# One transformer block in one pass: x^T of four tiles of the second half through VectorE and a DRAM scratch, and a different order on VectorE in the opening

## The chip, the core and the metric

The kernel runs on one core of a Trainium2 chip. A core has TensorE (PE, matmuls and transposes, results in PSUM), VectorE (DVE), ScalarE (ACT), GpSimd (POOL), and SyncE (SP), whose queue issues nearly all DMAs here. Each engine works through its own instructions in program order and waits where an operand is not there yet or a buffer is not free. The metric is the device time of one execution in microseconds (us); the median of three executions before the change is 1181.57 us (1181.06 to 1181.97).

## The reference, cut to what matters

```python
x = A_x                                  # 1 x 2048 x 576, fp32
xn = _layernorm(x)                       # over the 576 columns, eps 1e-5
# A: qkv = xn @ wqkv; 32 heads of 18; row s attends to rows s, s-2, ..., s-14 (8 of them)
# B: relu(xn @ w1) @ w2, 4608 hidden units
return x + softmax_attention(xn) @ wo + relu(xn @ w1) @ w2
```

The products have to hold fp32 accuracy. TensorE is fed in a shorter form (`F32R`), so every operand is split into a high part (the value rounded to F32R) and a low part (the value minus its high part), and a product is the sum high*high + low*high + high*low.

## The kernel before, in words

**Tiling.** Rows of even index are parity 0 and rows of odd index are parity 1 (an offset of 2 stays within a parity). Each parity (`ph`) has 8 tiles `i` of 128 rows; two tiles make a block `tb` of 256 rows. D = 576 columns are 4 pieces of 128 and a rest of 64. `XT[ph, tb]` holds x^T of a block as 9 pieces of 128 partitions: 4 high, 1 mixed (high part of the rest on partitions 0 to 63, its low part on 64 to 127), 4 low. `TERMS` lists the 14 pairs of pieces that a product over D needs.

**Steps.** The MLP is cut into slots: parity, 12 chunks of hidden units, 4 blocks, 3 units of 128 hidden columns, so 144 slots a parity and 288 in all. The main loop has one step per slot `n`. In each, TensorE first does `h_mm(n + 2)` (14 matmuls of 256 columns: hidden units of the slot two ahead), then what the table `todo` has for the step, then `o_mm(n)` (12 matmuls of 288 columns, summed over three slots in the PSUM pair `PO`); then come the entries of `todo_late`. `h_out` makes the relu's high part on ScalarE (`hhi`, L500) and its low part on VectorE (`hlo`, L503). After the third slot of a chunk `o_out` (L544) adds `PO` to the tile of x, which is also the accumulator of the output; after the last chunk the tile is written out (L474). The tables are written by hand, step by step; `run_bg` puts the attention's VectorE work between the steps by a small sum of expected PE and VectorE time.

**x^T by TensorE.** For a tile of x: `load_x` (a DMA), `stats` (bn_stats and two small ones on VectorE, L239 to L243, then `nm` and `rstd` on GpSimd, L244 and L245), `norm` (one VectorE instruction, L260, or two on ScalarE, L257 and L258), `make_xt`: five TensorE transposes of 128x128 or 128x64 into both buffers of the PSUM pool `ps_m` (L274, L275), then high part on ScalarE (L279), low part on VectorE (L282), and the same for the rest (L286, L289). For parity 1 this is spread over steps 129 to 153, with the last chunk of parity 0 starting at slot `e` = 132: tile `i` is loaded at step e - 3 + 2i, its statistics come late in e + 1 + 2i, its norm late in e + 2 + 2i and its transposes in e + 4 + 2i. That is 136, 138, 140 and 142 for tiles 0 to 3. `h_mm` of parity 1 begins in step 142 (slot 144, block 0) and reaches block 1 in step 145.

**The wo path.** The attention's result of a tile is turned without TensorE: `wo_a` transposes 32x32 blocks on VectorE (L430, L431) into `tr` and stores it in four DMAs to the DRAM tile `turned` (L437), so that the order of blocks is put right; `wo_f` fetches it (L444); `wo_s` splits it (L451 to L453); `wo_b` multiplies with wo in `ps_m` and adds to x (L466). For parity 0, tiles 5 to 7 of it are under way in steps 130 to 136; `wo_b` of tile 7 stands in step 136, ahead of the transposes of parity 1's tile 0.

**Weights.** `run_splits(n)` at the start of a step splits what is due (L137 on ScalarE, L139 or L141 on GpSimd or VectorE) and issues the next weight DMA, three ahead, in the same SP queue.

**The opening.** The first slots, and x^T of parity 0's eight tiles, are laid out by hand ahead of the loop, which starts at step 4. Tiles 4 and 5 are transposed around `h_terms(4)` and `h_terms(5)`. The table `HEAD` places tiles 6 and 7: statistics of 6 in step 4, norm of 6 and statistics of 7 late in step 4, norm of 7 in step 5 (both norms on ScalarE), transposes of 6 late in step 5 and of 7 in step 6. Both need both buffers of `ps_m`.

Of the kernel before, what the change touches and what calls it, by code (L numbers as in the profile page):

```python
# [17 lines left out]
P = 128  # L18
# [3 lines left out]
TBN = 256  # L22
# [5 lines left out]
EPS = 1e-5  # L28

UNIT0, UNIT_STEP, WO_AT = 7, 27, 8  # L30
WO_STEPS = (0, 1, 3, 4, 6, 7, 9, 10)
HEADW = (-9, -8, -7, -6, -5, -4)
FIRST = 4
# [2 lines left out]
    (4, 0, 'stats', 6),  # L36
    (4, 1, 'norm', 6, True),
    (4, 1, 'stats', 7),
    (5, 0, 'norm', 7, True),
    (5, 1, 'xt', 6),  # L40
    (6, 0, 'xt', 7),
)
HALO = ((0, 112), (112, 127))
WARM = 24

# [2 lines left out]
def tile_body(ctx: ExitStack, tc: tile.TileContext, x, wqkv, wo, w1, w2, out):  # L48
# [28 lines left out]
    lgp = pool("lgp", 2)  # L77
    smp = pool("smp", 2)
    tmp = pool("tmp", 2)
    turned = pool("turned", 3, space=bass.MemoryType.DRAM)  # L80
    ps_o = pool("ps_o", 2, space=PSUM)
    ps_h = pool("ps_h", 2, space=PSUM)
    ps_m = pool("ps_m", 2, space=PSUM)
# [145 lines left out]
    def stats(ph, i, parts=False):  # L229
        xt = X[ph, i]  # L230
        st = smp.tile([P, 2, 6], F32, name="bst")
        mv = smp.tile([P, 2], F32, name="mv", bufs=4)
        r = smp.tile([P, 1], F32, name="rstd", bufs=4)
        nm = smp.tile([P, 1], F32, name="nm", bufs=4)
        MR[ph, i] = nm, r

        def sums():
            for h in range(2):
                nc.vector.bn_stats(st[:, h, :], xt[:, h * D2 : (h + 1) * D2])  # L239

        def rest():
            nc.vector.bn_aggr(mv, st)
            nc.vector.tensor_scalar(mv[:, 1:2], mv[:, 1:2], EPS, None, op0=ALU.add)  # L243
            nc.gpsimd.tensor_scalar(nm, mv[:, 0:1], -1.0, None, op0=ALU.mult)  # L244
            nc.gpsimd.tensor_tensor(r, mv[:, 1:2], mhalf, op=ALU.pow)  # L245
            dve(700)

        if not parts:
            sums()
            rest()  # L250
        return sums, rest

    def norm(ph, i, act=False):
        nm, r = MR.pop((ph, i))
        xn = tmp.tile([P, 640], F32, name="xn", bufs=3)[:, 0:D]
        if act:
            nc.scalar.activation(xn, X[ph, i], AF.Identity, bias=nm)  # L257
            nc.scalar.activation(xn, xn, AF.Copy, scale=r)  # L258
        else:
            nc.vector.tensor_scalar(xn, X[ph, i], nm, r, op0=ALU.add, op1=ALU.mult)  # L260
            dve(600)
        XN[ph, i] = xn

    def transpose_split(src, hi, mix, lo, bank=None, parts=False):

        if bank is ps_o:
            po = ps_o.tile([P, 2, 512], F32, name="po")
            pa, pb = po[:, 0, :].rearrange("p (k c) -> p k c", k=KT), po[0:DR, 1, 0:P]
        else:
            pa = ps_m.tile([P, KT, P], F32, name="pm")  # L270
            pb = ps_h.tile([P, TBN], F32, name="ph") if bank is ps_h else ps_m.tile([P, P], F32, name="pm")
            pb = pb[0:DR, 0:P]
        for k in range(KT):
            nc.tensor.transpose(pa[:, k, :], src[:, k * P : (k + 1) * P], ident)  # L274
        nc.tensor.transpose(pb, src[:, KT * P : D], ident)  # L275
        t["pe"] += 5 * 0.06

        def high():
            nc.scalar.activation(hi, pa, AF.Copy)  # L279

        def low():
            nc.vector.tensor_tensor(lo, pa, f32(hi), op=ALU.subtract)  # L282
            dve(512)

        def last_high():
            nc.scalar.activation(mix[0:DR], pb, AF.Copy)  # L286

        def last_low():
            nc.vector.tensor_tensor(mix[DR:P], pb, f32(mix[0:DR]), op=ALU.subtract)  # L289
            dve(128)  # L290

        steps = high, low, last_high, last_low
        if not parts:
            for f in steps:
                f()
        return steps

    def make_xt(ph, i, bank=None, parts=False):
        tb, h = divmod(i, 2)
        if h == 0:  # L300
            XT[ph, tb] = xtp.tile([P, 9, TBN], F32R, name="xT")
        d = XT[ph, tb][:, :, h * P : (h + 1) * P]
        xn = XN.pop((ph, i))
        return transpose_split(xn, d[:, 0:4, :], d[:, 4, :], d[:, 5:9, :], bank, parts)


    TERMS = [(k, k) for k in range(KT)] + [(5 + k, k) for k in range(KT)] + [(4, 4)] + [(k, 5 + k) for k in range(5)]


    QO, KK, VV = {}, {}, {}  # L310
# [108 lines left out]

    OT = {}  # L420

    TD = {}

    def wo_a(ph, i):


        assert (ph, i) in ready, (ph, i, len(bg))
        o = QO[ph][:, i, :]
        tr = tmp.tile([P, 640], F32, name="tr", bufs=1)
        nc.vector.transpose(tr[:, 0:D], o)  # L430
        nc.vector.transpose(tr[:, D:640], o[:, KT * P : D])  # L431
        dve(D)
        dve(DR)
        TD[ph, i] = turned.tile([5 * 4, 32, P], F32, name="turned")
        for r in range(4):
            rows = slice(32 * r, 32 * r + 32)
            nc.sync.dma_start(  # L437
                TD[ph, i][:, :, rows].rearrange("g j i -> j g i"),
                tr[rows, :].rearrange("j (g i) -> j g i", i=32),
            )  # L440

    def wo_f(ph, i):
        OT[ph, i] = tmp.tile([P, 5, P], F32R, name="xn", bufs=3)
# [2 lines left out]
    def wo_s(ph, i):  # L446

        r = OT[ph, i]
        z = f32(r)
        d = tmp.tile([P, 5, P], F32R, name="oT", bufs=1)  # L450
        nc.scalar.activation(d, z, AF.Copy)  # L451
        nc.vector.tensor_tensor(r[:, 0:KT], z[:, 0:KT], f32(d[:, 0:KT]), op=ALU.subtract)
        nc.vector.tensor_tensor(d[DR:P, KT], z[DR:P, KT], f32(d[DR:P, KT]), op=ALU.subtract)  # L453
        dve(512)
        dve(128)
        OT[ph, i] = [d[:, k] for k in range(5)] + [r[:, k] for k in range(4)]

    def wo_b(ph, i):
        d, w = OT.pop((ph, i)), WO[ph]
# [56 lines left out]
    def o_mm(n, out=True):  # L516
        ph, c, tb, f = slots[n]
        hi, lo = H.pop(n)
        w = W2[ph, c, f]
        end = n == len(slots) - 1  # L520
        for k in range(2):
            if f == 0:
                PO[k] = ps_o.tile([P, 2, 512], F32, name="po")
            cs = slice(k * P, (k + 1) * P)
            terms = [(j, l, b, h) for j, (l, b) in enumerate(((hi, 0), (hi, 1), (lo, 0))) for h in range(2)]
            if end:
                terms.sort(key=lambda z: z[3])
            for j, l, b, h in terms:
                mm(
                    PO[k][:, h, 0:D2], l[:, cs], w[:, b, h * D2 : (h + 1) * D2],  # L530
                    f == 0 and j == 0, f == C - 1 and j == 2, D2,
                )
        if out:
            o_out(n)
# [23 lines left out]
    def at(n, f, *a):  # L558
        todo.setdefault(n, []).append((f, a))
# [3 lines left out]
    def late(n, f, *a):  # L563
        todo_late.setdefault(n, []).append((f, a))

    plan = []
    for ph in range(NPH):
        b = ph * SPP
        for c in range(NCH):
            for f in range(C):  # L570
                s = b + c * SPC + f
                first = ph == c == 0
                plan.append((HEADW[f] if first else s - 5, w1_task, ((ph, c, f), c * C + f)))
                plan.append((HEADW[3 + f] if first else s - 3, w2_task, ((ph, c, f), c * C + f)))
        for u in range(NU):
            s = b + UNIT0 + u * UNIT_STEP
            plan.append((s - 5, wq_tasks, ((ph, u), u)))
            for i in range(NI):
                at(s + i, qkv_tile, ph, u, i)
            late(s + NI + 1, attention, ph, u)  # L580
        s = b + UNIT0 + NU * UNIT_STEP + WO_AT
        plan.append((s - 8, wo_tasks, (ph,)))
        for i in range(NI):
            z = s + WO_STEPS[i]
            late(z, wo_a, ph, i)
            at(z + 1, wo_f, ph, i)
            late(z + 2, wo_s, ph, i)
            at(z + 3, wo_b, ph, i)
            at(z + 3, done, ph, i)
        if ph + 1 < NPH:  # L590
            e = b + SPP - SPC
            for i in range(NI):
                z = e + 3 + 2 * i
                at(z - 6, load_x, ph + 1, i)
                late(z - 2, stats, ph + 1, i)
                late(z - 1, norm, ph + 1, i)
                at(z + 1, make_xt, ph + 1, i)
    for step, f, a in sorted(plan, key=lambda z: z[0]):
        if f in (wq_tasks, wo_tasks):
            f([step + k for k in range(5)], *a)  # L600
# [56 lines left out]
    make_xt(0, 3, bank=ps_h)  # L657
    o_mm(2, out=False)
    stats(0, 4)
    stats(0, 5)  # L660
    h_mm(3)
    norm(0, 4)
    norm(0, 5)
    h_terms(4, TERMS)
    h4 = h_out(4, parts=True)
# [14 lines left out]
    for n in range(FIRST, len(slots)):  # L680
        run_splits(n)
        m = n + LAG
        if m < len(slots):
            h_mm(m)
        for f, a in todo.pop(n, []):
            f(*a)
        if n >= 0:
            o_mm(n)
        for f, a in todo_late.pop(n, []):
            f(*a)  # L690
        run_bg(M[slots[n][3] if n >= 0 else 0])
    assert not todo and not todo_late and not bg and not tasks and not staged

# [25 lines left out]
```

## Time and profile before

| what | value |
|---|---|
| median of three executions | 1181.57 us |
| profiled execution: time | 1181.42 us |
| profiled execution: span | 1179.7 us |
| TensorE busy | 1171.0 us, 8936 matmuls and transposes |
| VectorE busy | 818.8 us, 1298 instructions |
| ScalarE busy | 301.9 us, 738 instructions |
| GpSimd busy | 47.5 us |
| one TensorE transpose, 128x128 (L274) | 272 ns median |
| block transpose on VectorE, 128x576 (L430) | 778 ns median |
| granted TensorE clock | 1.0 |

A line of the chain of waits has start, length, engine, output tile and line. A line of the timeline has start, length (of the whole group when it ends in x2 and the like), engine, line, operation, output and input, shapes, and in brackets the idle time just before and what ended it. TensorE's matmuls overlap, so the spacing of starts says more of their cost than the length of one.

### The profile page before, as it was taken

How to read it: one execution, taken by the hardware profiler on the slowest of the kernel's cores; microseconds unless marked ns; L12 is line 12 of the kernel's file. 1: busy time of each engine (PE TensorE's matmuls, PEld its weight loads, DVE VectorE, ACT ScalarE, POOL GpSimd, SP SyncE). 2: the span in 40 equal slices, each digit the busy share in tenths (PEclk: the TensorE clock that was granted, in tenths of full speed). 3: DMA queues.
4: the chain of work that ended last, by engine and by line, in shares of the span. 5: the costliest groups of instructions: out<-in, count | busy, mean ns of one | idle time of the engine just before them, and what ended most of it. 6: DMA issues, size and time to landing. Idle time of an engine off the chain costs nothing.

```text
span 1179.7 us, 21695 instructions
## 1 busy us (share of the span) xinstructions
PE 1171.0 (99%) x8936; PEld 1162.3 (99%) x8936; DVE 818.8 (69%) x1298; ACT 301.9 (26%) x738; POOL 47.5 (4%) x70
## 2 busy tenths in 40 slices
PE   8999999999999999999999999999999999999998
PEld 8999999999999999999999999999999999999998
DVE  7427875888687678877673288758777884887752
ACT  5412222131222222321233123121222322222210
POOL 3200000010000000000020000000100000000000
PEclk9999999999999999999999999999999999999999
DMA  5312121130321211355342113030302313113431
GB/s 182 97 34 76 55 61 56 38 108 1 99 58 46 74 48 42 94 129 134 107 148 66 46 53 88 27 83 23 96 22 79 79 34 89 54 30 99 110 99 61
DMA packets 137650, 86.15 MB, mean 73 GB/s; under 512 B 48864, under 2 KB 121312, under 8 KB 137552
## 3 DMA queue, kind: packets, MB, share of 16 engines
q1 hardware_dynamic: 134736, 76.28, 23.7%
q10 hardware_dynamic: 2816, 8.49, 2.5%
q8 instruction: 70, 1.15, 0.4%
q14 instruction: 28, 0.23, 0.1%
HBM read 66.58 MB, written 9.96 MB: 65 GB/s over the span
## 4 chain that ended last, share of the span: by engine, by line
PE 96%; DVE 1%; DMA 1%; ACT 0%; issue 0%; POOL 0%; SPq 0%; DVEq 0%; ACTq 0%; POOLq 0%
PE ph L105 38%; PE po L105 38%; PE pm L105 20%; PE pm L274 0%; DVE bst L239 0%; DMA xn<-turned 0%; DMA x<-in_x 0%; DMA st<-in_wqkv 0%; DMA turned<-tr 0%; DVE pr L395 0%; POOL rstd L245 0%; DVE w2t L141 0%; ACT xn L257 0%; DVE hlo L503 0%; DVE x L550 0%
## 5 line engine op out<-in xcount | busy, mean ns | idle before, releaser
L105 PE MATMUL ph<-xT,w1t 128*128 128x256 f32 x4018 | 509.3, 278 | 0.7 <-ACT xT L279 0.7
L105 PEld LDWEIGHTS ph<-xT,w1t 128*128 128x128 f32 x4018 | 489.1, 188 | 1.1 <-ACT xT L279 1.0
L105 PE MATMUL po<-w2t,hhi 128*128 128x288 f32 x2304 | 400.7, 296 | 0.0
L105 PEld LDWEIGHTS po<-w2t,hhi 128*128 128x128 f32 x2304 | 337.0, 188 | 1.0
L500 ACT ACTIVATE hhi<-ph 128x256 fp32r<-128x256 f32 x287 | 109.9, 383 | 583.4 <-PE ph L105 560.2
L105 PE MATMUL po<-w2t,hlo 128*128 128x288 f32 x1152 | 245.0, 293 | 0.0
L503 DVE SCALAR_TENSOR_TENSOR hlo<-ph,hhi 128x256 fp32r<-128x256 f32 x287 | 120.8, 421 | 169.2 <-ACT hhi L500 168.5
L544 DVE TENSOR_TENSOR x<-po,x 128x576 f32<-128x576 f32 x190 | 142.5, 756 | 67.2 <-PE po L105 64.1
L105 PE MATMUL pm<-wq,xT 128*128 128x432 f32 x896 | 185.5, 358 | 0.0
L105 PEld LDWEIGHTS po<-w2t,hlo 128*128 128x128 f32 x1152 | 183.8, 188 | 0.0
L105 PEld LDWEIGHTS pm<-wq,xT 128*128 128x128 f32 x896 | 163.8, 188 | 5.6
L358 DVE TENSOR_TENSOR pr<-qo,k 128x1152 f32<-128x1152 f32 x64 | 85.8, 1348 | 0.0
L361 DVE TENSOR_REDUCE lg<-pr 128x64 f32<-128x1152 f32 x64 | 84.9, 1342 | 0.0
L388 DVE TENSOR_TENSOR pr<-lg,v 128x1152 f32<-128x1152 f32 x64 | 84.6, 1348 | 0.2
L141 DVE TENSOR_TENSOR w2t<-st,w2t 128x576 fp32r<-128x576 f32 x72 | 54.3, 754 | 40.4 <-ACT w2t L137 40.2
L395 DVE TENSOR_TENSOR pr<-pr 128x288 f32<-128x288 f32 (+1 forms) x128 | 70.4, 598 | 0.1
L141 DVE TENSOR_TENSOR w1t<-st,w1t 128x640 fp32r<-128x640 f32 x70 | 57.3, 818 | 12.1 <-ACT w1t L137 12.0
L137 ACT ACTIVATE w2t<-st 128x576 fp32r<-128x576 f32 x72 | 49.3, 685 | 55.1 <-PE po L105 46.5
L327 ACT ACTIVATE k<-pm 128x144 f32<-128x144 f32 x64 | 18.6, 291 | 146.5 <-PE pm L105 146.5
L137 ACT ACTIVATE w1t<-st 128x640 fp32r<-128x640 f32 x72 | 52.9, 735 | 2.5 <-DMA st<-in_w 2.3
L364 POOL TENSOR_SCALAR_AFFINE_SELECT lg<-lg 1x512 f32<-1x512 f32 x8 | 9.4, 1172 | 836.7 <-DVE lg L361 836.7
L105 PE MATMUL pm<-wq,oT 128*128 128x288 f32 x224 | 35.2, 296 | 0.8 <-ACT oT L451 0.8
(71 smaller groups left out, 444.2 us busy)
## 6 DMA issues: line engine op xcount, KB each, us to landing
st<-in_w SPq DMA_DIRECT2D x72, 288.0 KB, 3.0
st<-in_w SPq DMA_DIRECT2D x72, 256.0 KB, 3.1
st<-in_wqkv SPq DMA_DIRECT2D x32, 216.0 KB, 3.1
turned<-tr SPq DMA_DIRECT2D x64, 80.0 KB, 2.2
xn<-turned SPq DMA_DIRECT2D x16, 320.0 KB, 3.3
st<-in_w SPq DMA_DIRECT2D x144, 32.0 KB, 2.8
x<-in_x SPq DMA_DIRECT2D x15, 288.0 KB, 4.4
out<-x SPq DMA_DIRECT2D x14, 288.0 KB, 2.2
```

The lines of the kernel that those rows point to most:

```text
L105: nc.tensor.matmul(o, l, r, start=start, stop=stop)
L137: nc.scalar.activation(hi, src, AF.Copy)
L141: nc.vector.tensor_tensor(lo, src, f32(hi), op=ALU.subtract)
L327: nc.scalar.activation(k[:, W - 1 + i, :], pq[:, 1, :], AF.Copy)
L358: nc.vector.tensor_tensor(pr[i], q, window(k, i), op=ALU.mult)
L361: nc.vector.tensor_reduce(lg[:, i], pr.pop(i).rearrange(heads, d=Dh), axis=AX.X, op=ALU.add)
L364: nc.gpsimd.affine_select(out=z, in_=z, pattern=[[1, NI], [1, W], [0, HG]], compare_op=ALU.is_ge, fill=-1e9 / scale, base=1 - W, channel_m ...
L388: nc.vector.tensor_tensor(pr[i].rearrange(heads, d=Dh), e, window(v, i).rearrange(heads, d=Dh), op=ALU.mult)
L395: nc.vector.tensor_tensor(o, z[:, 0:n], z[:, n : 2 * n], op=ALU.add)
L500: nc.scalar.activation(hi, pt, AF.Relu)
L503: nc.vector.scalar_tensor_tensor(lo, pt, 0.0, f32(hi), op0=ALU.max, op1=ALU.subtract)
L544: nc.vector.tensor_tensor(acc, PO[k][:, :, 0:D2], acc, op=ALU.add)
```

## The change

Tiles 0 to 3 of parity 1 get their own steps (`XT_STEPS`, relative to e = 132): load, statistics, norm (now two ScalarE instructions, into half of a product buffer `pr`), block transposition on VectorE into the other half with four stores to a DRAM tile, fetch by three DMAs straight into the piece positions of `XT`, and the split in place. The five TensorE transposes of these four tiles go. To let the fetch land in pieces 0 to 3, high and low parts change places in `XT`, and `TERMS` is renumbered; the order of high and low products stays the same. In the opening, `norm(0, 4)` moves ahead of `h_mm(3)`, between the two halves of `stats(0, 5)`; the norm of tile 7 goes from ScalarE in step 5 to VectorE late in step 4; and in step 5 the second of `o_out`'s two additions moves behind the split of tile 6's transposes.

```diff
+XT_STEPS = (
+    (-6, 0, 1, 2, 4, 7),
+    (-5, 1, 2, 3, 5, 8),
+    (-3, 2, 3, 4, 6, 10),
+    (3, 4, 5, 6, 8, 11),
+)
@@
-    (5, 0, 'norm', 7, True),
+    (4, 1, 'norm', 7),
     (5, 1, 'xt', 6),
     (6, 0, 'xt', 7),
 )
+HALVED = 5
@@
-    turned = pool("turned", 3, space=bass.MemoryType.DRAM)
+    turned = pool("turned", 4, space=bass.MemoryType.DRAM)
@@
-        return transpose_split(xn, d[:, 0:4, :], d[:, 4, :], d[:, 5:9, :], bank, parts)
-    TERMS = [(k, k) for k in range(KT)] + [(5 + k, k) for k in range(KT)] + [(4, 4)] + [(k, 5 + k) for k in range(5)]
+        return transpose_split(xn, d[:, 5:9, :], d[:, 4, :], d[:, 0:4, :], bank, parts)
+    TERMS = (
+        [(5 + k, k) for k in range(KT)] + [(k, k) for k in range(KT)] + [(4, 4)]
+        + [(5 + k, 5 + k) for k in range(KT)] + [(4, 9)]
+    )
+
+    def blocks_out(td, tr):
+        for r in range(4):
+            rows = slice(32 * r, 32 * r + 32)
+            nc.sync.dma_start(
+                td[:, :, rows].rearrange("g j i -> j g i"),
+                tr[rows, :].rearrange("j (g i) -> j g i", i=32),
+            )
+
+    def norm_turned(ph, i):
+        nm, r = MR.pop((ph, i))
+        z = prp.tile([P, W, UD], F32, name="pr").rearrange("p w c -> p (w c)")
+        XN[ph, i] = xn, _ = z[:, 0:D], z[:, D : 2 * D]
+        nc.scalar.activation(xn, X[ph, i], AF.Identity, bias=nm)
+        nc.scalar.activation(xn, xn, AF.Copy, scale=r)
+
+    def xt_a(ph, i):
+        xn, tr = XN.pop((ph, i))
+        nc.vector.transpose(tr, xn)
+        dve(D)
+        TD[ph, i] = turned.tile([D // 32, 32, P], F32, name="words")
+        blocks_out(TD[ph, i], tr)
+
+    def xt_f(ph, i):
+        tb, h = divmod(i, 2)
+        if h == 0:
+            XT[ph, tb] = xtp.tile([P, 9, TBN], F32R, name="xT")
+        z, td = f32(XT[ph, tb][:, 0:5, h * P : (h + 1) * P]), TD.pop((ph, i))
+        nc.sync.dma_start(z[:, 0:KT], td[0 : 4 * KT].rearrange("(k c) j i -> (c j) k i", k=KT))
+        for rows in slice(0, DR), slice(DR, P):
+            nc.sync.dma_start(z[rows, KT], td[4 * KT : D // 32].rearrange("c j i -> (c j) i"))
+
+    def xt_s(ph, i):
+        tb, h = divmod(i, 2)
+        d = XT[ph, tb][:, :, h * P : (h + 1) * P]
+        z = tmp.tile([P, 5, P], F32R, name="oT", bufs=1)[:, 0]
+        mix = d[:, 4, :]
+        nc.scalar.activation(d[:, 5:9, :], f32(d[:, 0:4, :]), AF.Copy)
+        nc.vector.tensor_tensor(d[:, 0:4, :], f32(d[:, 0:4, :]), f32(d[:, 5:9, :]), op=ALU.subtract)
+        nc.scalar.activation(z[DR:P], f32(mix[DR:P]), AF.Copy)
+        nc.vector.tensor_tensor(mix[DR:P], f32(mix[DR:P]), f32(z[DR:P]), op=ALU.subtract)
+        nc.scalar.activation(mix[0:DR], f32(mix[0:DR]), AF.Copy)
+        dve(512)
+        dve(128)
@@
             for i in range(NI):
-                z = e + 3 + 2 * i
-                at(z - 6, load_x, ph + 1, i)
...
+                if i >= len(XT_STEPS):
...
+                load, first, second, send, back, parts = (e + k for k in XT_STEPS[i])
+                at(load, load_x, ph + 1, i)
+                late(first, stats, ph + 1, i)
+                late(second, norm_turned, ph + 1, i)
+                late(send, xt_a, ph + 1, i)
+                at(back, xt_f, ph + 1, i)
+                at(parts, xt_s, ph + 1, i)
@@
     stats(0, 4)
-    stats(0, 5)
+    s5 = stats(0, 5, parts=True)
+    s5[0]()
+    norm(0, 4)
     h_mm(3)
-    norm(0, 4)
+    s5[1]()
     norm(0, 5)
     h_terms(4, TERMS)
@@
         if n >= 0:
-            o_mm(n)
+            o_mm(n, n != HALVED)
+        if n == HALVED:
+            o_out(n, (0,))
         for f, a in todo_late.pop(n, []):
             f(*a)
+        if n == HALVED:
+            o_out(n, (1,))
```

`wo_a` now calls `blocks_out` with the same four stores as before, and `wo_s` hands its pieces to `wo_b` in the new numbering.

More of the change, by code (lines that the diff above doesn't have):

```diff
@@ L310, in tile_body @@
+    TD = {}
     QO, KK, VV = {}, {}, {}
@@ L420, in tile_body @@
     OT = {}
-    TD = {}
     def wo_a(ph, i):
@@ L434, in wo_a @@
         TD[ph, i] = turned.tile([5 * 4, 32, P], F32, name="turned")
[L435 to L440, printed above, removed]
+        blocks_out(TD[ph, i], tr)
     def wo_f(ph, i):
@@ L455, in wo_s @@
         dve(128)
-        OT[ph, i] = [d[:, k] for k in range(5)] + [r[:, k] for k in range(4)]
+        OT[ph, i] = [r[:, k] for k in range(KT)] + [d[:, KT]] + [d[:, k] for k in range(KT)]
     def wo_b(ph, i):
@@ L592, in tile_body @@
             for i in range(NI):
-                z = e + 3 + 2 * i
-                at(z - 6, load_x, ph + 1, i)
-                late(z - 2, stats, ph + 1, i)
-                late(z - 1, norm, ph + 1, i)
-                at(z + 1, make_xt, ph + 1, i)
+                if i >= len(XT_STEPS):
+                    z = e + 3 + 2 * i
+                    at(z - 6, load_x, ph + 1, i)
+                    late(z - 2, stats, ph + 1, i)
+                    late(z - 1, norm, ph + 1, i)
+                    at(z + 1, make_xt, ph + 1, i)
+                    continue
+                load, first, second, send, back, parts = (e + k for k in XT_STEPS[i])
[5 more added lines that the diff above has]
+                at(parts, xt_s, ph + 1, i)
     for step, f, a in sorted(plan, key=lambda z: z[0]):
```

## The prediction

> **What bounds the kernel now.** First I read the page: busy shares, chain of waits, DMA issues.
>
> ```profile
> PE 1171.0 (99%) x8936; PEld 1162.3 (99%) x8936; DVE 818.8 (69%) x1298; ACT 301.9 (26%) x738; POOL 47.5 (4%) x70
> ...
> PE 96%; DVE 1%; DMA 1%; ACT 0%; issue 0%; POOL 0%; SPq 0%; DVEq 0%; ACTq 0%; POOLq 0%
> ...
> turned<-tr SPq DMA_DIRECT2D x64, 80.0 KB, 2.2
> xn<-turned SPq DMA_DIRECT2D x16, 320.0 KB, 3.3
> ```
>
> TensorE is busy almost throughout, at a granted clock of 1.0 in every slice, and 96% of the chain is its own. So an instruction less on TensorE is time gained, if nothing that replaces it makes TensorE wait; work on other engines costs nothing until it is late. The last two rows price the detour the four tiles will take: a store of this shape lands 2.2 us after issue, a fetch 3.3 us.
>
> Next, the chain over the end of parity 0 (start, length).
>
> ```profile
> 559.02 1.61 PE ph L105 x14
> ...
> 565.94 1.60 PE ph L105 x14
> ...
> 571.17 0.47 DVE x L466
> ...
> 571.68 0.66 PE pm L274 x4
> 572.33 0.11 PE pm L275
> ...
> 574.03 1.61 PE ph L105 x14
> ...
> 577.23 1.61 PE ph L105 x14
> 578.85 0.44 PE pm L274 x4
> 579.28 0.11 PE pm L275
> ...
> 580.99 1.61 PE ph L105 x14
> ```
>
> Each "ph" line begins a step: 135 at 559.02, 136 at 565.94, 137 at 574.03, 138 at 577.23, 139 at 580.99. Step 137 has no transposes and takes 3.20 us; step 138 has tile 1's and takes 3.76. So five transposes cost 0.56 us on the path, not their listed 5 x 0.27, because they overlap. Steps 135 and 136 hold the same matmuls, but 136 also has tile 0's transposes: 8.09 against 6.92, so these cost 1.17. The extra 0.6 is a wait: the transposes need both `ps_m` buffers, which VectorE's addition of wo's product (L466) still holds.
>
> Last, the opening, VectorE and TensorE by timeline.
>
> ```profile
> 22.46 0.21 DVE L242 BATCH_NORM_AGGREGATE mv<-bst 128x2 f32<-128x12 f32 x1
> ...
> 23.11 1.23 DVE L260 TENSOR_SCALAR xn<-x,nm,rstd 128x576 f32<-128x576 f32 x2
> 24.25 0.75 DVE L544 TENSOR_TENSOR x<-po,x 128x576 f32<-128x576 f32 x1
> 25.12 0.69 DVE L282 TENSOR_TENSOR xT<-pm,xT 128x512 fp32r<-128x512 f32 x1
> ```
>
> ```profile
> 23.83 0.63 PE L274 MATMUL pm<-ident,xn 128*128 128x128 f32 x4 [0.17 <-DVE xn L260]
> ...
> 26.06 0.60 PE L274 MATMUL pm<-ident,xn 128*128 128x128 f32 x4
> ...
> 37.41 0.65 PE L274 MATMUL pm<-ident,xn 128*128 128x128 f32 x4 [0.48 <-DVE xT L282]
> ```
>
> TensorE waits a little for the norm of tile 4 at 23.83, not at tile 5 (26.06), and 0.48 us at tile 7 (37.41), for the low part of tile 6.
>
> **Term 1: the transposes that go.** Tile 0: 1.17. Tiles 1 to 3, by steps 138, 140 and 142 (3.76, 3.75, 3.75 against 3.20): 0.56 + 0.55 + 0.55. Sum -2.83 us, if the new path is hidden. TensorE's next work after `wo_b` of tile 7 is `o_mm(136)`, which uses the other PSUM pool, so tile 0's wait has no successor there.
>
> **What hides the new path.** New work per tile: two ScalarE instructions for the norm (0.78 each, L257 and L258) for one on VectorE (0.58), a block transpose on VectorE (0.78 by L430, the same 576 columns), four stores, three fetches, and one or two short ScalarE copies more. VectorE is 8.5 us busy in the 16 us from 550, ScalarE 2.6. I follow the queues, in the old clock less what is already saved.
>
> - Tile 0: transposed after the split of wo's tile 6, about 560.8 to 561.5. SP issues its stores behind two output DMAs, 562.1 to 564.8 (0.68 each, as the group at 550.17: 2.74 for four); landed at 567. Fetch issued by 571, landed 574.3. Split due in step 139, about 581.
> - Tile 2's norm writes the `pr` buffer that tile 0's stores read, so ScalarE waits until 567, with the `hhi` of slot 138 behind it: ready at 568.9 instead of 567.6. The slot's low part must be done before `h_mm(140)` takes that PSUM buffer at 576.1: some 7 us to spare.
> - Tile 1: stored 567.0 to 569.7, landed 572. Its fetch stands behind tile 2's stores (572.8 to 575.5) in SP's queue, is issued by 576.8 and lands at 580. Split in step 140 (584 to 586); first reader `h_mm(144)` at 588.9 (591.14 less 2.28).
> - Tile 3: its load waits for tile 0's output DMA as before; stores to 582.4, fetch landed 589.7, split at 594, first reader `h_mm(147)` at 599.0.
> - Queued behind these on SP: the weight load of step 139, 578.4 before, about 582.4 to 584.1 now, landed 587. Its split opens step 141 at 585.7, so ScalarE waits some 1.3 us, with `hhi` of slot 143 behind it, which `o_mm(143)` needs near 592. Hidden.
>
> Cost taken: 0. From below nothing is to be gained; from above the bound is the rival of late data.
>
> **Term 2: norm 4 ahead, a loss.** TensorE's wait at 23.83 goes: the transposes of tile 4 follow the matmuls at 23.67 and end at 24.22 in the chain's clock, where they ended at 24.56. But VectorE now does: norm 4 at 22.45 (`rstd` of tile 4 ends at 22.42), `hlo` of slot 3 at 22.95, and only then the aggregate of tile 5 at 23.28 instead of 22.46. GpSimd follows 0.37 later (as 21.30 to 21.67) and takes 0.76 for `nm` and `rstd`: 24.41. Norm 5 starts at 24.44, where it started at 23.75. Behind it stand the first addition of `o_out(2)` (24.94) and the low part of tile 4, 25.62 to 26.31. Tile 5's transposes want `ps_m` at about 25.7 and get it 0.06 later than this: 26.37. Begun after a wait they take 0.65 + 0.11 in the chain (as at 37.41), so `o_mm(3)` starts at 27.13, where it started at 26.77. **+0.36 us.** From below, if norm 5 gates nothing: -0.34.
>
> `rstd` of tile 5 took 0.77 before, beside VectorE's norm 4, against 0.57 for tiles 4, 6 and 7; in the new order VectorE idles while it runs, so I take 0.57. The Trainium skill, "SBUF — State Buffer", section "SBUF: two separate sides", has VectorE and GpSimd share a port pair by an exclusive lock, so that the loser blocks for a whole instruction. That agrees with 0.77 and 1.04 beside VectorE's work; with 0.77 here too the term would be +0.56.
>
> **Term 3: norm 7 to VectorE, additions split around tile 6: a gain.** ScalarE spends 34.51 to 36.1 on norm 7 while tile 6's transposes are finished at 35.2; its high part starts at 36.05, the low part at 36.66, and TensorE gets `ps_m` at 37.41. New: norm 7 on VectorE at 33.93 (`rstd` ends 33.90), in a stretch where VectorE idles 1.48 us. High part of tile 6 at 35.23 to 35.82; on VectorE one addition (34.98 to 35.66), then the low part 35.85 to 36.54. TensorE finishes `h_mm(8)` at 36.68 and goes straight on: 35.15 + 1.61 + 0.55 = 37.31 for the start of `o_mm(6)`, against 38.17. **-0.86 us.** The second addition then ends at 37.6, and `o_mm(6)` needs its buffer at 38.1. If it frees nothing: 0.
>
> **Sum.** -2.83 + 0.36 - 0.86 = -3.33 us. The profiled span 1179.7 would become 1176.4, its time 1181.42 would become 1178.1; that execution lies 0.15 below the median, so for the median **1178.2 us**.
>
> **Rivals.**
>
> - *Norm 5 gates nothing* (tile 4's low part is ready sooner than I place it): -2.83 - 0.34 - 0.86 = -4.03, 1177.5. For it: only 0.6 us decides. Against: VectorE is in order, norm 5 ahead.
> - *Tile 7 still waits*: its slack is 0.1 us, and a stall that moves to the second addition would take the place of the one removed. -2.83 + 0.36 = -2.47, 1179.1.
> - *The new path is a little late*: the tightest reader is `h_mm(144)`, 3 us behind tile 1's split; ScalarE, in order, is stopped by a buffer or a weight load for some us too long. 1 to 4 us of TensorE waiting end between 1179.2 and 1182.2.
> - *Slower: the stores land late.* One mechanism, in step 135: ScalarE stops at tile 2's norm until tile 0's stores have landed, and `hhi` of slot 138 stands behind. With landing time L, ScalarE goes on at 564.8 + L, and needs 1.56 for the norm, 0.38 for `hhi`, VectorE 0.42 for `hlo`, by 576.1: TensorE waits from L = 8.9 us on, and the change is a loss above 8.9 + 3.3 = 12.2. At L = 16 it is 1181.57 - 3.33 + 7.1 = 1185.3. For it: the pieces are short; 48864 packets lie under 512 B already, mostly these stores (2560 a tile by 16 tiles is 40960). Against: 64 such stores landed in 2.2 median, 3.7 at most. The Trainium skill, "VectorE: DVE Perf Modes", section "The three transpose paths", warns that a plain DMA which transposes by strides is 19 times slower than the transposing one, and in "Rules for kernel authors" recommends TensorE for 128x128; by 19 x 2.2, an estimate, L would be 42 and the loss some 30 us. The row speaks against it: the same pattern already lands in 2.2, since the blocks are turned in VectorE.
>
> That the change does not do what it says is hardly open: 20 transposes leave TensorE, 8936 becomes 8916.
>
> **Chances.** Forecast 55%, its own range 1177.8 to 1178.8 (term 2 to 0.56, measurement). Norm 5 gates nothing 13%, tile 7 still waits 12%, path a little late 14%, slower 6%. What this kernel's measurement can tell from no change is about 0.2%, 2.4 us: below 1179.2 is faster, above 1183.9 slower. The first three cases are faster (80%), the fourth nearly all the same (14%), the last slower (6%). For 8 in 10 the range takes the first three and the start of the fourth: 1177.0 to 1180.3.
>
> **What would show it.** Steps 136, 138, 140 and 142 as long as their neighbours (6.92 and 3.20) and no TensorE wait for the split of `xT` from step 142 on: term 1. An idle gap before tile 5's transposes near 26.4, named for tile 4's low part: term 2. Tile 7's transposes directly behind `h_mm(8)`: term 3. I am wrong if TensorE's waits name ScalarE between steps 136 and 147, or if the landing of the new stores is far above 2.2.

## The result, and the profile after

| | before | after |
|---|---|---|
| median of the comparison | 1181.57 us (1180.92 to 1182.19, 22 runs) | 1179.91 us (1179.09 to 1180.99, 22 runs) |
| profiled execution: time, span | 1181.42, 1179.7 us | 1179.64, 1177.8 us |

The kernel is faster by 1.66 us, ratio 0.9986 [0.998, 0.9993]. The forecast was 1178.2, a gain of 3.33: half of it arrived. The time lies inside the forecast's range (1177.0 to 1180.3), outside the likeliest case's own (1177.8 to 1178.8).

The page of the changed kernel, in the lines that answer to those of before:

```profile
PE 1168.6 (99%) x8916; PEld 1159.7 (98%) x8916; DVE 819.5 (70%) x1299; ACT 307.7 (26%) x748; POOL 46.8 (4%) x70
...
PE 93%; DMA 2%; SPq 2%; DVE 2%; issue 0%; ACT 0%; POOL 0%; DVEq 0%; ACTq 0%; POOLq 0%
...
turned<-tr SPq DMA_DIRECT2D x64, 80.0 KB, 2.7
xn<-turned SPq DMA_DIRECT2D x16, 320.0 KB, 3.1
```

The 20 transposes are gone (8916) and TensorE's busy time fell by 2.4 us. But its share of the chain fell from 96% to 93%: transfers and SP's queue now stand in it with 2% each. That is a sign of where to look, not of how much was lost (2% are some 23 us).

The end of parity 0, by TensorE's timeline after the change (the `h_mm` that begins steps 138 to 141, and 144):

```profile
575.63 1.78 PE L113 MATMUL ph<-xT,w1t 128*128 128x256 f32 x14
...
578.83 1.78 PE L113 MATMUL ph<-xT,w1t 128*128 128x256 f32 x14
...
582.03 1.78 PE L113 MATMUL ph<-xT,w1t 128*128 128x256 f32 x14
...
585.23 1.78 PE L113 MATMUL ph<-xT,w1t 128*128 128x256 f32 x14
...
594.83 1.78 PE L113 MATMUL ph<-xT,w1t 128*128 128x256 f32 x14
```

Each step is 3.20 us, the three from 585.23 to 594.83 (9.60) too; steps 138, 140 and 142 took 3.75 before. No wait of TensorE for the split of x^T shows here. What follows step 143, by the chain of waits of the same kernel:

```profile
595.03 0.15 DVE hlo L555
595.18 0.18 issue
595.36 0.68 DVE xT L359
596.08 0.29 DVE xT L361
596.40 0.77 DVE x L596
597.17 0.14 issue
597.30 1.84 PE po L113 x12
```

The next `o_mm`, of slot 144, starts at 597.30 only when the addition of step 143 (L596) has freed its buffer. That addition stands on VectorE behind the low parts of tile 3 (L359, L361). In the execution shown this costs about 0.4 us.

The opening after the change, VectorE by timeline:

```profile
22.26 0.58 DVE L268 TENSOR_SCALAR xn<-x,nm,rstd 128x576 f32<-128x576 f32 x1
...
24.16 0.58 DVE L268 TENSOR_SCALAR xn<-x,nm,rstd 128x576 f32<-128x576 f32 x1 [0.69 <-POOL rstd L253]
24.66 0.75 DVE L596 TENSOR_TENSOR x<-po,x 128x576 f32<-128x576 f32 x1
25.33 0.68 DVE L290 TENSOR_TENSOR xT<-pm,xT 128x512 fp32r<-128x512 f32 x1
```

And TensorE's transposes of tiles 4, 5 and 7:

```profile
23.28 0.60 PE L282 MATMUL pm<-ident,xn 128*128 128x128 f32 x4
...
26.07 0.66 PE L282 MATMUL pm<-ident,xn 128*128 128x128 f32 x4 [0.48 <-DVE xT L290]
...
36.83 0.60 PE L282 MATMUL pm<-ident,xn 128*128 128x128 f32 x4
```

The waits for tiles 4 and 7 are gone, and one for tile 5 has come, named for tile 4's low part: VectorE idles 0.69 us for `rstd` of tile 5, and an addition and that low part stand behind.

To place the rest, the start of each slot's `hhi` on ScalarE marks the same point in every kernel. Shift against the profile of before, in us (negative is a gain); all twelve experiments are listed, and described below. "End" is the time from the last `hhi` to the end of the span in the trace, unrounded (1179.67 us before, 1177.85 after); it is 8.50 before. From slot 9 to 120 and from 147 to 260 nothing shifts.

```
            to slot 3  opening  wo, parity 0  turn of parity  wo, parity 1   end
                        3..9      120..136       136..147       260..276
after         -0.21    -0.43      +0.40          -2.48          +0.10       9.28
e1            -0.07     0.00      +0.08          -2.87          +0.25       8.65
e2            -0.35    -0.43      +0.01          -0.01          -0.90       8.70
e3            +0.07    -0.42      -0.02          -2.86          -0.10       9.29
e4            -0.05    -1.14      +0.14          -2.86          -0.17       9.29
e5            +0.36    -0.38      +0.92          -2.86          +0.13       8.63
e6            +0.02    -1.07      +0.42          -2.86          -0.15       8.64
e7            -0.07    -0.41      +0.39          -2.86          +0.51       9.31
e8            +0.06    +0.06      +0.27          -1.21          -0.65       8.47
e9            -0.39    -0.45      +0.19          -2.48          -0.02       9.30
e10           +0.07    -1.07      +0.08          -2.82          +0.38       8.63
e11           +0.11    -1.07      +0.05          -2.86          +0.11       9.25
e12           +0.28    -0.10      +0.46          -0.01          -0.88       9.24
```

For the changed kernel: -0.21 - 0.43 + 0.40 - 2.48 + 0.10 + (9.28 - 8.50) = -1.84, within rounding the 1.82 by which its span is shorter. Two columns in which I had written nothing hold a loss: the wo stretch of parity 0, ahead of the place where the four tiles are turned, and the end. The wo stretch of parity 1 holds one as well, hidden because the profile of before has a wait there too, of another cause (below). (I take the first column for chance: the changed kernel itself stands at -0.21 and, as e3, at +0.07.)

### The profile page after: what moved, and what is told of

Read it like the earlier page. It is cut to its first block, busy times and chain, and to the rows that moved or that the text cites. A ratio compares the mean times of both kernels' runs of the same rounds, so it can differ in the third digit from the quotient of the medians.

```text
span 1177.8 us, 21712 instructions
## 1 busy us (share of the span) xinstructions
PE 1168.6 (99%) x8916; PEld 1159.7 (98%) x8916; DVE 819.5 (70%) x1299; ACT 307.7 (26%) x748; POOL 46.8 (4%) x70
## 4 chain that ended last, share of the span: by engine, by line
PE 93%; DMA 2%; SPq 2%; DVE 2%; issue 0%; ACT 0%; POOL 0%; DVEq 0%; ACTq 0%; POOLq 0%
PE po L113 36%; PE ph L113 36%; PE pm L113 19%; SPq L323 1%; DMA xn<-turned 1%; DMA turned<-tr 1%; DMA st<-in_w 0%; DVE pr L454 0%; PE pm L282 0%; DMA st<-in_wqkv 0%; DMA x<-in_x 0%; DVE x L596 0%; DVE tr L487 0%; SPq L350 0%; ACT oT L503 0%
## 5 line engine op out<-in xcount | busy, mean ns | idle before, releaser
L596 DVE TENSOR_TENSOR x<-po,x 128x576 f32<-128x576 f32 x190 | 142.4, 755 | 67.2 <-PE po L113 64.1
```

The lines of the kernel that those rows point to most:

```text
L596: nc.vector.tensor_tensor(acc, PO[k][:, :, 0:D2], acc, op=ALU.add)
```

## The experiments

The edits are shown against the changed kernel, except the last. Each time is a median against that of the kernel before in the same comparison. The question behind all of them: is the missing half lost in the parts themselves, in a neighbouring stretch, or at the end?

**The four tiles alone**, with the opening undone.

```diff
-    (4, 1, 'norm', 7),
+    (5, 0, 'norm', 7, True),
-HALVED = 5
+HALVED = -1
@@
-    s5 = stats(0, 5, parts=True)
-    s5[0]()
-    norm(0, 4)
+    stats(0, 5)
     h_mm(3)
-    s5[1]()
+    norm(0, 4)
     norm(0, 5)
```

> Only the new path of x^T for tiles 0 to 3 of parity 1; the opening as before. Theory A (the path is worth 2.4 us in its own stretch: 2.83 of TensorE time less 0.39 where slot 144 waits for the additions of step 143; what the whole change lost besides is lost in the wo stretch of parity 0, where an earlier TensorE runs into a store and fetch that are not earlier): -2.4 us on the kernel before, about 1179.1, step 129's wo product without a wait, and the 0.39 at slot 144 still there. Rival B (the path itself costs more than its stretch shows, in the landing of the output or in DMA traffic): -1.7 or less, 1179.9 or more, with the last output transfer landing about 0.7 later than before.

Measured: 1178.91 against 1181.06, -2.15 us, 0.9983 [0.9974, 0.9992]. The turn of the parity gives 2.87, 0.04 more than the working's 2.83, so the step that saves works as forecast. The 0.39 at slot 144, which theory A kept, is not in this profile, and the median lies between theory A's -2.4 and rival B's -1.7.

**The opening alone.**

```diff
-XT_STEPS = (
-    (-6, 0, 1, 2, 4, 7),
...
-)
+XT_STEPS = ()
```

> Only the new order of the opening; x^T of parity 1 by TensorE as before. Theory A: 0.4 us is gained by step 7, and about as much is lost again in step 129, since TensorE there comes earlier to a wo tile whose fetch is not earlier; 1181.2 to 1181.6, no difference that can be measured. Rival B (the gain of the opening stays): 1181.1 or less.

Measured: 1180.28, -0.78 us, 0.9992 [0.9984, 1.0001]; the interval just reaches 1. The opening gives 0.43 and the gain is still there behind slot 120. One theory was that a TensorE that comes earlier merely runs into a wo fetch that does not come earlier; here it loses 0.01 in that stretch.

**The changed kernel again**, beside the two.

> The changed kernel once more, unchanged, to see what of its profile repeats. If the gap at slot 144 (0.4 us) and the wait in step 129 repeat and the time from the last DMA issue to the end does not (3.6 in the first profile against 2.9 before), the latter is chance; if that repeats too, it belongs to the change. Time 1179.6 to 1180.2.

Measured: 1179.08, -1.98 us, 0.9982 [0.9973, 0.9991]. Its profile has no loss at slot 144 and none in the wo stretch, but the long end (9.29). The two parts alone make -2.93 together, 0.95 more than the whole; the ends account for 0.44 of it (+0.15 and +0.20 against the whole's +0.79). The rest I can't assign; medians of the same kernel differ by 0.3 between comparisons (-1.66 and -1.98).

**Tile 5's wait taken away**: an addition of `o_out(2)` that stood behind norm 5 moves ahead of it, into the time in which VectorE waits for `rstd`.

```diff
     s5[1]()
+    o_out(2, (0,))
     norm(0, 5)
...
-    o_out(2, (0,))
```

> The changed kernel with one line moved in the opening: the first addition of o_out(2) ahead of norm 5 on VectorE, so that it fills the 0.7 us in which VectorE waits for the rstd of tile 5. The prediction's term 2: tile 5's transposes then follow at about 25.6 without a wait, and o_mm(3) starts 0.5 to 0.6 earlier. Theory A: this does not reach the end, because step 129 waits already: 0 to -0.2 us against the changed kernel, and the wait of TensorE for the split of the wo tile grows by as much. Rival B: -0.5 to -0.6 us all the way.

Measured: 1178.53, -2.53 us, 0.9979 [0.997, 0.9988]; in the same comparison 0.55 less than the changed kernel, and 0.72 less in the opening column. VectorE by timeline of this kernel:

```profile
23.55 0.75 DVE L596 TENSOR_TENSOR x<-po,x 128x576 f32<-128x576 f32 x1
24.32 0.58 DVE L268 TENSOR_SCALAR xn<-x,nm,rstd 128x576 f32<-128x576 f32 x1
24.82 0.68 DVE L290 TENSOR_TENSOR xT<-pm,xT 128x512 fp32r<-128x512 f32 x1
```

The addition fills the idle time, and the low part starts 0.5 us earlier (25.33 before this edit). Tile 5's transposes start at 25.65 without a wait. That confirms the cause named in term 2. Since this gain from the opening also reaches the end, the theory of the wo fetch falls a second time.

**Two small ScalarE instructions more, at the start**, to shift where in the kernel ScalarE's code is loaded. The reason lies in the transfers of the last 4.5 us of the span, in 40 slices; first the changed kernel:

```profile
GB/s 0 0 0 0 0 225 328 348 287 369 348 389 348 328 317 390 307 348 389 348 133 31 21 20 31 10 0 0 0 0 0 0 0 0 0 0 0 0 0 0
...
q14 instruction: 1, 0.01, 0.5%
...
out<-x SPq DMA_DIRECT2D x2, 144.0 KB, 2.1
out<-x ACTq DMA_DIRECT2D x2, 144.0 KB, 2.2
```

Then the kernel before:

```profile
GB/s 0 0 0 0 0 0 0 0 0 0 0 164 317 317 328 349 348 348 420 338 328 338 307 348 369 420 185 21 0 0 0 0 0 0 0 0 0 0 0 0
...
out<-x SPq DMA_DIRECT2D x2, 144.0 KB, 1.8
out<-x ACTq DMA_DIRECT2D x2, 144.0 KB, 1.8
```

The four last outputs go over 16 DMA engines. After the change a packet of an instruction queue (q14) falls among them; the bulk is through by slice 20, but five slices follow at 10 to 31 GB/s, some 0.6 us in which a small remainder drains. Before there is no such packet, and the rate drops at once. As an estimate, one of 16 engines moves 348 / 16 = 22 GB/s of the full rate, so the tail looks like a remainder on about one engine; which engine a packet is on, the trace does not say.

```diff
+    for _ in range(2):
+        nc.scalar.activation(spare, mhalf, AF.Exp)
```

> The changed kernel with two more tiny ScalarE instructions (128x1, in the first 4 us, where ScalarE waits for x), so that ScalarE's instruction stream is two longer, as with the old opening. Theory C (the end of the changed kernel is 0.6 to 0.7 us longer because one 8 KB packet of the instruction queue falls among the last output packets; its moment hangs on ScalarE's instruction count): the last packet of that queue moves more than 10 us ahead of the end, the time from the last hhi to the end falls from 9.25 to about 8.6, and the median is 0.6 us lower than the changed kernel's (1179.08 in the runs before on this kind of chip). Rival D (the longer landing belongs to the new DRAM tiles or to chance): no change.

Measured: 1179.44 against 1181.32, -1.88 us, 0.9982 [0.9974, 0.9991]. The packet moved to 10.5 us ahead of the end, and the end is 8.63. But the time does not show it: this execution lost 0.92 in the wo stretch instead, and the median is no better than that of the changed kernel. In time the run settles nothing.

**Both of these edits together.**

> The two mends together: the first addition of o_out(2) ahead of norm 5, and two more tiny ScalarE instructions. Theory C with additive parts: 0.7 from the opening and 0.65 from the end, 1.3 us under the changed kernel, about 1177.8, some 3.2 us under the kernel before. Rival D: 1178.5 as with the opening alone.

Measured: 1178.47, -2.85 us, 0.9974 [0.9963, 0.9985]; opening -1.07, end 8.64. Against the kernel before this is 0.32 more than the first edit alone gave in another comparison (-2.53), half of the 0.65 that theory C added: the time decides for neither side.

**Tile 3's split later**: from ahead of `o_mm(143)` to the end of that step.

```diff
-                at(parts, xt_s, ph + 1, i)
+                (late if i == 3 else at)(parts, xt_s, ph + 1, i)
```

> The changed kernel with tile 3's split put behind the two additions of step 143 on VectorE. If the gap of 0.4 us at slot 144 in the first profile is a standing cost of the change (split and late weights ahead of the additions that free PO), the median falls by up to 0.4. If it is chance, from a weight load that landed in 4.1 us once, the median stays within 0.2 of the changed kernel and no gap is seen at slot 144.

Measured: 1179.42, -1.90 us, 0.9983 [0.9974, 0.9992]. The stretch is at -2.86, without the wait at slot 144, yet the median did not move. Only 2 of the 10 profiles with four tiles (the changed kernel's first and e9's) had that wait, so it is not a standing cost of the kernel.

**Only tile 0 on the new path**, opening undone, in a single execution.

```diff
 XT_STEPS = (
     (-6, 0, 1, 2, 4, 7),
-    (-5, 1, 2, 3, 5, 8),
-    (-3, 2, 3, 4, 6, 10),
-    (3, 4, 5, 6, 8, 11),
 )
```

> Opening as before and the new path for tile 0 alone; tiles 1 to 3 by TensorE. The prediction's term 1: step 136 shrinks from 8.09 to 6.92 us, 1.17 in all, as the wait for wo's additions has no successor. Rival: the wait moves to tile 1 or to the next use of the buffers, and only the 0.55 of the five transposes is gained.

Measured: span 1178.2, time 1179.99. The turn of the parity gives 1.21, where the forecast had 1.17 for this tile: here the transpose group that also waits for PSUM is worth twice one that does not (0.55).

**The loads of x at their old steps.** The change moves three loads of x from steps 129, 131 and 133 to 126, 127 and 129, among the wo stores and fetches of parity 0.

```diff
-    (-6, 0, 1, 2, 4, 7),
-    (-5, 1, 2, 3, 5, 8),
-    (-3, 2, 3, 4, 6, 10),
+    (-3, 0, 1, 2, 4, 7),
+    (-1, 1, 2, 3, 5, 8),
+    (1, 2, 3, 4, 6, 10),
```

> The changed kernel with the loads of tiles 0 to 2 back at their old steps (129, 131, 133 in place of 126, 127, 129); all else as changed. Theory E (the earlier loads, put into SP's queue ahead of the wo path's stores and fetches, make the fetch of a wo tile land late and TensorE wait between slots 126 and 137; eight profiles with the new path lose 0.02 to 0.93 us there, 0.3 on average, the two without it 0): no TensorE wait for oT before slot 138, and a median 0.2 to 0.4 us below the changed kernel's, 2.2 to 2.4 below the kernel before. Rival F (the stores and fetches of the new path do it, or chance): the waits stay and the median with them.

Measured: 1179.43 against 1181.58, -2.15 us, 0.9984 [0.9975, 0.9993], just short of theory E's 2.2, and 0.19 is still lost in the wo stretch. SP's timeline shows what a load of x does to the wo path. The changed kernel:

```profile
521.93 0.52 SPq L235 DMA_DIRECT2D x<-in_x  x1
522.55 3.22 SPq L323 DMA_DIRECT2D turned<-tr  x4
...
528.03 0.38 SPq L496 DMA_DIRECT2D xn<-turned  x1
```

The kernel before:

```profile
522.93 2.18 SPq L437 DMA_DIRECT2D turned<-tr  x4
...
526.93 0.38 SPq L444 DMA_DIRECT2D xn<-turned  x1
```

With the loads back at their old steps:

```profile
522.30 2.05 SPq L323 DMA_DIRECT2D turned<-tr  x4
...
526.26 0.38 SPq L496 DMA_DIRECT2D xn<-turned  x1
```

The changed kernel once more (e3):

```profile
521.46 0.52 SPq L235 DMA_DIRECT2D x<-in_x  x1
522.71 2.23 SPq L323 DMA_DIRECT2D turned<-tr  x4
...
527.22 0.38 SPq L496 DMA_DIRECT2D xn<-turned  x1
```

With a load of x (L235) right ahead of them, the four stores of a wo tile take 3.22 us to issue instead of 2.18; in e3, where they begin 0.7 us after the load, 2.23. The fetch that needs them goes out late in both: from the first store to the fetch 4.50 to 5.48 us pass in the eight profiles with all three early loads, 3.62 to 4.19 in the six others. But TensorE's wait at this place is not for that fetch. The chain of the changed kernel has TensorE behind the fetch of the tile before, which was issued at 521.48, ahead of the load at 521.93:

```profile
521.48 3.72 DMA xn<-turned
...
525.31 0.75 ACT oT L503
526.06 0.04 issue
526.11 3.97 PE pm L113 x28
```

**Everything together**: old loads, tile 5's addition, the two ScalarE instructions; and **the same without the ScalarE instructions**.

> Three mends together: loads at the old steps, the first addition of o_out(2) ahead of norm 5, two more tiny ScalarE instructions. With additive parts: opening 1.14, middle 2.86, no loss in the wo stretch, the end as short as before: 4.0 us under the kernel before. If the end's 0.6 us does not show in runs without a profile, as e5's median suggests, 3.4.

> As e10 but without the two tiny ScalarE instructions. Theory C: 0.6 us slower than e10, its last instruction packet again among the output packets. If the packet costs only in the profile: the same median as e10.

Measured: 1178.43, -3.15 us, 0.9974 [0.9964, 0.9984], and 1179.15, -2.43 us, 0.9979 [0.9971, 0.9988]. Between them, in one comparison, lie 0.72 us by the two instructions alone, as 0.62 lie between their ends (8.63 and 9.25). Theory C holds here, though single runs overlap (1178.03 to 1179.14 and 1178.41 to 1179.78). The first has the largest gain of all, but stays short of both its forecasts (4.0 and 3.4). The transfers of its last 4.5 us, where no instruction packet falls:

```profile
GB/s 0 0 0 0 0 0 0 0 0 0 51 266 328 317 338 328 369 358 389 328 338 328 338 369 369 348 82 0 0 0 0 0 0 0 0 0 0 0 0 0
```

The low tail is gone, as in the kernel before.

**The early loads alone, in the kernel before.**

```diff
-                at(z - 6, load_x, ph + 1, i)
+                at((e - 6, e - 5, e - 3)[i] if i < 3 else z - 6, load_x, ph + 1, i)
```

> The kernel before with nothing changed but the loads of tiles 0 to 2 of parity 1, moved to steps 126, 127 and 129 as in the change. Theory E: TensorE waits for oT between slots 126 and 137, and the median is 0.2 to 0.4 us above the kernel before. Rival F: no difference.

Measured: 1182.09, +0.51 us, 1.0006 [0.9997, 1.0015]; the interval holds 1. The wo stretch loses 0.46, but 0.29 of it by slot 129, where TensorE's wait ends before the first moved load is issued, as TensorE's and SP's timelines show:

```profile
509.81 1.32 PE L105 MATMUL pm<-wq,oT 128*128 128x288 f32 x8 [0.20 <-ACT oT L451]
```

```profile
511.43 0.52 SPq L227 DMA_DIRECT2D x<-in_x  x1
```

Only the other 0.17 can be the loads'. The end is long too (9.24), with two packets of the instruction queue in the last 4.5 us though no ScalarE instruction was added; so ScalarE's code is not the only one whose loading can fall there.

## Why the prediction was half right

**Term 1 was right.** Forecast -2.83; of the ten profiles with four tiles six show -2.86, one -2.87, one -2.82, and two -2.48 with the wait at slot 144. Tile 0's 1.17 measured 1.21. The queues went as followed in the working: behind ScalarE's stop at tile 2's norm, `hhi` of slot 138 was ready at 568.5 (forecast 568.9), and SP issued the weight load of step 139 from 583.74 (forecast 582.4). All of this stayed hidden.

**Term 2 was right in mechanism and nearly in size.** The wait at 26.07, named for tile 4's low part, stands where the working put it (26.37, less the 0.21 by which this execution's head was early). Slots 3 to 6 lost 0.28 against the forecast 0.36. `rstd` of tile 5 took 0.57 with VectorE idle, as assumed.

**Term 3 was right, a little too large:** 0.71 against 0.86. I took the arrival of TensorE at tile 7 from a timeline start (36.76 in the working's clock); the chain's clock, 0.16 later for the same transposes of tile 5 (26.22 against 26.06), gives 36.92. Together the two terms gave -0.43 for the forecast -0.50.

**The step that failed is "What hides the new path … Cost taken: 0".** I followed SP's queue from tile 0's transposition at 560 us to the split of tile 3, and there it holds, but for the 0.35 at slot 144 in two of ten profiles. What the change adds and takes away is also felt outside that stretch. The largest cost of this kind lies in the wo stretch of parity 1, at 1082 to 1091 us (below). A smaller one may lie ahead of 560 us, where three loads of x move 3, 4 and 4 steps ahead, past wo stores and fetches of parity 0. Of that stretch's loss, what is gone by slot 129 (up to 0.39) comes before the first moved load. From slot 129 to 136 the changed kernel loses 0.37, e5 0.70, e12 0.17, e6 0.10, and the nine other experiments nothing: four of the eight profiles with all three early loads, 0.17 us in their mean, and none of the six others. In the changed kernel even this wait is for a fetch issued ahead of the load beside it. So the loads delay the wo path, but that TensorE pays for it is not shown, and the times don't show it either: e11 differs from e4 by its old loads alone, and their medians, from two comparisons, are -2.43 and -2.53.

**A second term was left out of the sum: the end.** The seven profiles with an instruction packet in their last 4.5 us have an end of 9.24 to 9.31, the seven others, before among them, 8.47 to 8.70. In the mean this is 0.7 us; e10 against e11 shows it in the time as well, e5 does not. It has nothing to do with the change's purpose: a kernel with a few more or fewer instructions, or with some in another place (e12), has its code loaded at other moments.

For the profiled executions the account closes: 1.49 us less gain than forecast are 0.35 at slot 144, 0.07 in the opening, 0.40 and 0.10 in the two wo stretches and 0.78 at the end, less the 0.21 won by chance at the head.

**The wo stretch of parity 1 holds a cost of its own.** All ten profiles with four tiles wait there 0.7 to 1.4 us for a wo tile; e2, e8 and e12 wait 0.2 at most and stand 0.65 to 0.90 better than before. The kernel before waited too, by TensorE's timeline, here ahead of the changed kernel's line:

```profile
1093.20 1.33 PE L105 MATMUL pm<-wq,oT 128*128 128x288 f32 x8 [0.83 <-ACT oT L451]
```

```profile
1090.62 1.32 PE L113 MATMUL pm<-wq,oT 128*128 128x288 f32 x8 [0.95 <-ACT oT L503]
```

The two waits have different causes. SP's timeline shows the four stores of that tile, in the kernel before and in the changed one:

```profile
1084.83 2.06 SPq L437 DMA_DIRECT2D turned<-tr  x4
```

```profile
1082.12 2.87 SPq L323 DMA_DIRECT2D turned<-tr  x4
```

They take 2.71 to 3.39 us in the ten and 2.06 in before, e2, e8 and e12; from the first store to the fetch 4.51 to 5.01 us pass in the ten, 3.71 to 3.77 in the four. In before it was the fetch that landed late, 3.8 us after its issue where e2, e8 and e12 have 3.0 to 3.1:

```profile
xn<-turned SPq DMA_DIRECT2D x1, 320.0 KB, 3.8
```

In each of the ten, one of the four issues takes 1.1 to 1.9 us, and beside it runs a packet of the other instruction queue, q8; in the four there is none during the stores. From the list of transfers of the changed kernel, 1082 to 1085 us:

```profile
q8 instruction: 1, 0.02, 2.0%
```

The 70 packets on q8 stand against 17872 matmuls and weight loads before, one for about 255 of them, so they seem to carry TensorE's code. Taking out 20 transposes with their weight loads moves that code's loading against the wo stores: before, the packet began at 1083.72, ahead of the stores; now at 1083.06, among them. This explains why all ten are alike, but no edit has moved the packet alone, so it is argued and not shown. The mean wait is 0.95 in the ten and 0.25 in the other four: some 0.7 us of the median's shortfall may lie here, if those four stand for the kernel before, and 0.9 if its late fetch was chance.

**The rivals.** "Norm 5 gates nothing" falls by the 0.48 us at 26.07. "Tile 7 still waits" falls by 36.83, which has no wait. "The path a little late" came true in part: a wait of 0.4 at slot 144 in two of ten profiles, but for a buffer behind the split and not for x^T. That the measured time lies inside the range is therefore partly luck: the range reached up to 1180.3 for this rival, and the costs that took the time there are others. "The stores land late" is far off, by the list of DMA issues of the changed kernel:

```profile
words<-pr SPq DMA_DIRECT2D x16, 72.0 KB, 2.8
xT<-words SPq DMA_DIRECT2D x4, 256.0 KB, 3.9
```

The new stores land after 2.8 us, where TensorE would wait from 8.9 on. The 19-fold cost in the Trainium skill, "VectorE: DVE Perf Modes", section "The three transpose paths", did not appear; the page means a DMA that transposes by its strides, and here VectorE has turned the blocks before they are stored.

## What to carry to other kernels

A step that is moved takes its DMAs with it: follow each of them from its new place, not from where the new computation begins; here the moved loads made the way from a wo tile's stores to its fetch 0.9 us longer in the mean. Before a wait is put down to them, see which transfer it is for, and whether that was issued before or after. Taking instructions out of an engine's program may also move the loading of its code, and what runs beside it, far from the place of the edit. When an engine must wait for a short result of another one (here 0.69 us for `rstd`), the next instruction that does not need it belongs ahead of the wait; that was worth 0.55 us and cost nothing. Before a gain of a tenth of a per cent is credited or denied to an edit, compare the last microseconds of the two spans, since they moved by 0.6 to 0.7 us with two instructions that compute nothing of the result.

## What was not expected of the hardware

An instruction queue's packet of about 8 KB (0.25 MB in 30 on q14) lengthens the last output transfers from 1.8 to 2.1 or 2.2 us (medians of two; the later one of each pair takes 2.5 instead of 1.8 or 1.9), and the whole end by 0.7 in the mean, when it falls among them. The Trainium skill, "Runtime: NRT & Kernel Launch", section "Instruction fetch mechanics", says that the sequencer fetches the next block by a DMA queue of its own while the current one runs, and counts this as mostly hidden. Here it is not hidden from the transfers that it falls among; that these wait on the packet's own DMA engine is inferred from the rate of the tail alone.

The time that SP needs for one DMA issue of the same shape is not constant: four stores took 2.05 to 3.39 us in the places compared above, mostly because single issues of some 1 to 1.86 us stand among those of 0.5. The traces say where most of these stand: over the 14 profiles 252 of the 269 issues on SP of more than 1 us run beside a packet of q8, and 443 of the 6472 shorter ones. The long stores of 522 us, right behind a load of x, are among the 17 others. Why a packet of one queue holds up an issue on another was not found.
